# A gated mix of an S4 convolution and a dense layer, forward and backward, on one core: the order of the work around K's reload

## The chip, the cores and the metric

The kernel runs on one core of one Trainium2 chip. The metric is the time of one execution on the device, in microseconds (us). The engines are PE (matrix products; PEld is its weight load), DVE and ACT (elementwise work, and copies out of PSUM), POOL and SP (here almost only issuers of DMAs). Three queues issue DMAs: SP's, ACT's and POOL's. Each engine works through its own instructions in order.

## The reference

For a sequence `u` of 2048 rows of 448 channels the forward pass is a gate times a long convolution plus one minus the gate times a two-layer dense network, and the outputs are this result and the gradients of all inputs and weights:

```python
K = jnp.einsum("dn,dnl,dn->dl", Cc, P, dB).real      # P = exp(dt*A*l), 448 channels, 256 states, 2048 positions
Yf = rfft2(up) * rfft2(Kp)                           # zero-padded to 4096
y  = irfft2(Yf)[:L] + u * Dskip
h  = relu(x @ w1 + b1) ** 2
b  = h @ w2 + b2
out = g * y + (1 - g) * b                            # g = sigmoid(sum(u * gate_w))
_out, _vjp = jax.vjp(f, ...); grads = _vjp(grad_out)
```

## The kernel before

*FFT stage.* `u` and the gated gradient are transformed in two stages with matrix products: `fwd1` (line 222) writes its product to the DRAM buffer `gd`, `load_s1` reads it back transposed, `fwd2` (line 245) makes a spectrum, kept in DRAM as `sp_d`. `cmul` multiplies two spectra, `inv1` (line 272) is the first inverse stage and writes to `hd`; `load_hs` reads `hd` back, and `inv2` is the second inverse stage. `evac2` copies each product out of PSUM, half on ACT and half on DVE, or all on ACT while `act_only` is set. Between these, `powers` makes the tables from which K is built. A scheduler orders the instructions of this stage.

*Dense steps.* The dense layers are a generator (`dense`, line 896) of 196 steps: the first layer (`hidden`, `turn`, `mul_1`, 14 blocks of 128 features, four steps each), the second layer backward, the transposes of w1, and two projections (`project`, line 854: 16 rows of tiles, each in two half steps of 7 products, for each of two projections). `N_(n)` takes n steps; `D_(want)` takes steps until their summed costs reach `want`. The list `cost` gives each step a number.

*Chunks.* From line 957 on the order is the order of the code. K and its gradients are made in 14 chunks of 32 channels. A chunk is a list of tokens (`PERIOD`, line 1236): `YS`, `Y0` to `Y4` build a table Y on DVE, `KM` multiplies it on PE into 32 channels of K (`kgen`), `KO` copies them out and, after the last chunk, writes them to DRAM (`k_d`), `LY` transposes Y with four DMA transposes on SP, `X0` to `X2` build the other table, `Z0` to `Z3` are products on PE with the chunk before's transposed Y, each copied out by one ACT instruction, `P0` and `P1` products on DVE, `S` sums them on PE (`back_s`, 128 products into the PSUM tile psS) and writes them to `s_d` after every second chunk through a buffer `st`, `SA` and `WD` prepare weights. `D` stands for dense steps: the cost between the loop's start (`base`) and its end (`goal`) is spread evenly over all chunks, so that the last dense step runs just ahead of the last chunk's `KM`.

*Reload and tail.* After the last chunk `reload_k` loads K from `k_d` in rows by rounded position, 16 DMAs alternating between ACT's and POOL's queues. The small `fix` DMAs overwrite single rows of the `reload` ones and wait for them. `again` copies further rows on DVE. K then goes through `fwd1` (into `gd[2]`, with six stage buffers: four in the tile XB, two `st`), `load_s1`, `fwd2`; `product(w, q)` on DVE multiplies K's spectrum with that of the gradient (w = 0) or of `u` (w = 1), loaded from `sp_d` by `load_sx`, and `back1` is `inv1` of it, with four further stage buffers in the tile F. The products alternate between the tiles Pt and XB (`Pk`). A generator `param_grads` makes the parameter gradients in eight pieces for each of four channel blocks, taken by `Pg(n)`; its first block writes its results into XB. Two output loops end the kernel: out_0 (with `G`, the rows of grad_out, in the tile Y), and out_1.

Before the change the order at the end is: last `KM`, `KO`, `LY`, `P0`, `SA`, `reload_k`, `P1`, `S` of chunk 12, `WD`; loads of three spectra and of G's rows on SP; `Z0` to `Z3` of the last chunk (13); `again`; `P0`, `P1`; `fwd1` of K with the last chunk's sums between its parts; load of the constant `M2` into the tile M; `load_s1`.

## Time and profile before

| | |
|---|---|
| median of 3 runs | 879.25 us (879.04 to 881.17) |
| profiled execution | 882.18 us |
| its span, first to last instruction | 879.9 us |
| instructions | 20270 |
| busy share of the span: PE, PEld, DVE, ACT, POOL | 74%, 38%, 64%, 59%, 18% |
| mean granted clock of PE | 0.854 |
| moved by DMA | 181.58 MB, mean 206 GB/s |
| share of 16 DMA engines: SP's queue, POOL's, ACT's | 61.6%, 13.2%, 6.8% |

The profile is of one execution. Busy time is summed over instructions; PE's is partly modelled, since products are pipelined. In a row of the timeline come start and length in us, the engine (SPq and POOLq are the queues' own issuing work), the line, the operation, what it writes and reads, how many were merged (x), and in brackets how long the engine had stood before it and what ended that. The chain of waits gives start, length and what was waited for or done, followed back from the last instruction.

### The profile page before, as it was taken

What the parts mean: (1) busy time and instruction counts of PE and PEld (TensorE: products, weight loads), DVE (VectorE), ACT (ScalarE), POOL (GpSimd) and SP (SyncE); (2) the same over time, 40 slices, a digit from 0 to 9 for tenths busy, and PEclk for the clock granted to TensorE, in tenths of its full rate; (3) what the DMA queues carried; (4) which work ended last, traced back from release to release, by engine and by line L of the source; (5) the groups of instructions that cost most, each with busy time, mean ns of one, the idle gap of its engine ahead of it and who ended that gap; (6) DMA issues with size and microseconds to landing.
All of it is one profiled execution on the core that took longest, in us unless ns stands there. A gap on an engine that the chain in (4) does not pass through costs nothing.

```text
span 879.9 us, 20270 instructions
## 1 busy us (share of the span) xinstructions
PE 649.1 (74%) x8477; PEld 337.8 (38%) x8477; DVE 566.2 (64%) x932; ACT 515.5 (59%) x869; POOL 154.7 (18%) x260
## 2 busy tenths in 40 slices
PE   3578858777389987899999967988999151646382
PEld 1122323222244653556665643544656130323020
DVE  4595777975613573898889845475779151656574
ACT  1596787774166674587778737575454042656153
POOL 3122111105032011012111110100001132024142
PEclk9878976688699998999999986998999666879556
DMA  9957677587694889989998694985994997959892
GB/s 185 234 159 243 231 248 277 200 321 189 141 240 105 207 185 204 200 244 218 183 220 172 154 257 110 203 168 147 208 204 113 122 256 244 372 164 309 259 295 63
DMA packets 209545, 181.58 MB, mean 206 GB/s; under 512 B 132159, under 2 KB 185992, under 8 KB 209198
## 3 DMA queue, kind: packets, MB, share of 16 engines
q1 hardware_dynamic: 187822, 125.53, 61.6%
q0 software_dynamic: 13120, 34.18, 13.2%
q10 hardware_dynamic: 8512, 20.59, 6.8%
q8 instruction: 66, 1.08, 0.5%
q14 instruction: 25, 0.20, 0.1%
HBM read 85.19 MB, written 64.32 MB: 170 GB/s over the span
## 4 chain that ended last, share of the span: by engine, by line
PE 36%; DMA 19%; issue 15%; DVE 13%; ACT 12%; SPq 2%; POOL 2%; ACTq 0%; POOLq 0%; DVEq 0%
PE psN L876 8%; PE psN L683 5%; PE psN L647 5%; PE psS L1136 3%; PE psX L1064 3%; PE psF L1108 2%; DMA U<-rT_d 2%; DMA K<-dk_d 2%; DMA F<-rec_d 2%; PE psN L674 1%; DMA F<-k_d 1%; PE psN L650 1%; ACT U L675 1%; DMA K<-in_grad_out_dram 1%; DMA gd<-X 1%
## 5 line engine op out<-in xcount | busy, mean ns | idle before, releaser
L1110 ACT CAST P<-psF 128x1024 bf16<-128x1024 f32 x56 | 57.1, 1020 | 34.9 <-DMA F<-k_d 22.0
L1108 PE MATMUL psF<-S,R 41*128 41x32 bf16 x1792 | 32.0, 175 | 36.3 <-ACT P L1110 24.9
L683 PEld LDWEIGHTS <-U 128*128 128x128 bf16 x448 | 41.3, 101 | 39.5 <-issue 10.1
L647 PE MATMUL psN<-S 128*128 128x512 bf16 x168 | 48.2, 411 | 6.2 <-ACT st L1171 3.3
L683 PE MATMUL psN<-S,U 128*128 128x449 bf16 x224 | 51.3, 374 | 0.0
L1000 DVE TENSOR_TENSOR F<-Y,F 128x1024 bf16<-128x1024 bf16 (+3 forms) x70 | 47.2, 675 | 6.2 <-ACT F L1029 6.2
L999 DVE TENSOR_TENSOR Y<-Y,F 128x1024 bf16<-128x1024 bf16 (+3 forms) x70 | 48.0, 685 | 2.9
L1002 DVE TENSOR_TENSOR Y<-Y,F 128x1024 bf16<-128x1024 bf16 (+3 forms) x70 | 48.1, 687 | 2.4
L647 PEld LDWEIGHTS <-S 128*128 128x128 bf16 x336 | 30.1, 100 | 48.3 <-issue 22.2
L1108 PEld LDWEIGHTS <-R 41*128 41x128 bf16 x1792 | 27.4, 94 | 48.5 <-issue 39.8
L675 ACT ACTIVATE U<-psN 128x1024 bf16<-128x1024 bf16 x41 | 42.2, 1030 | 0.7 <-PE psN L674 0.7
L876 PE MATMUL psN<-D,U 128*128 128x448 bf16 x168 | 40.6, 395 | 2.6 <-ACT U L861 2.6
L876 PEld LDWEIGHTS <-U 128*128 128x128 bf16 x308 | 29.5, 103 | 33.2 <-issue 8.0
L662 ACT ACTIVATE U<-psN,b_f 128x512 bf16<-128x512 f32 x44 | 28.9, 685 | 19.3 <-PE psN L650 8.4
L989 DVE TENSOR_TENSOR R<-R,F 128x1024 bf16<-128x1024 bf16 (+1 forms) x14 | 13.4, 958 | 36.3 <-ACT R L1021 36.1
L1143 POOL DMA_DIRECT2D s_d<-st x28 | 14.5, 522 | 123.9 <-ACT st L1141 117.4
L253 PEld LDWEIGHTS <-M 128*64 128x64 bf16 x192 | 14.0, 127 | 55.2 <-issue 52.2
L647 PE MATMUL psN<-K,S 128*128 128x512 bf16 x126 | 33.3, 393 | 1.0 <-ACT R L768 0.7
L1119 DVE TENSOR_TENSOR M<-P,X 128x2048 bf16<-128x2048 bf16 x14 | 17.1, 1222 | 25.8 <-ACT P L1110 25.8
L1041 DVE COPY Y<-rec 128x256 bf16<-128x256 bf16 x14 | 10.2, 732 | 32.7 <-DMA K<-DBT_d 23.2
L1136 PE MATMUL psS<-ident,P 128*64 128x128 bf16 x896 | 28.3, 221 | 2.9 <-issue 2.9
L989 DVE TENSOR_TENSOR X<-X,F 128x1024 bf16<-128x1024 bf16 (+1 forms) x14 | 13.4, 959 | 23.4 <-ACT X L1021 21.1
(356 smaller groups left out, 1707.0 us busy)
## 6 DMA issues: line engine op xcount, KB each, us to landing
sp<-K ACTq DMA_DIRECT2D x8, 896.0 KB
R<-hd SPq DMA_DIRECT2D x14, 448.0 KB, 12.2
U<-rT_d SPq DMA_DIRECT2D x6, 896.0 KB, 5.9
hd<-F SPq DMA_DIRECT2D x11, 448.0 KB, 10.1
U<-rT_d SPq DMA_DIRECT2D x9, 512.0 KB, 6.4
X<-gd SPq DMA_DIRECT2D x5, 896.0 KB, 6.4
U<-dhT_d SPq DMA_DIRECT2D x5, 896.0 KB, 6.3
rT_d<-U POOLq DMA_DIRECT2D x8, 512.0 KB, 3.9
```

Source lines behind the costliest of these rows:

```text
L647: T_.matmul(pss[k][:], lhsT=w[:, dt], rhs=x(2 * half + k)[:, dt], start=(dt == 0), stop=False, skip_group_check=True)
L662: S.activation(r[:, 512 * lb:512 * lb + 512], pss[k][:], ACT.Relu, bias=b1_f[:, j:j + 1])
L675: S.activation(hn[j % 2][:, 8 * th:8 * th + 8, :], ps[:], f)
L683: T_.matmul(ps[:, 0:w], lhsT=hn[j % 2][:, t, :], rhs=rhs[:, t, :], start=(t == 0), stop=(t == LT - 1))
L876: T_.matmul(ps[:, 0:D], lhsT=src[:, j, P * x:P * x + P], rhs=ws[:, j, :], start=(w == 1 and j == 0), stop=(j == FT - 1))
L989: V.tensor_tensor(out=run(xb, 128 * n, [2048, 2], [W2, 2 * n], [1, W2]), in0=lo, in1=run(rx_[:, 0:1], 512 + W2 * k, [0, 2], [0, 2 * n], [1 ...
L999: V.tensor_tensor(out=run(yb, dst, [64, X2], [d0[1], n // d0[1]], [1, d0[1]]), in0=run(yb, 0, [64, X2], *src), in1=pr, op=ALU.mult)
L1000: V.tensor_tensor(out=run(vb, 0, [n, X2], [d0[1], n // d0[1]], [1, d0[1]]), in0=run(yb, 0, [64, X2], *src), in1=pi, op=ALU.mult)
L1002: return V.tensor_tensor(out=hi, in0=hi, in1=run(vb, n, [2 * n, W2], [-n, 2], [1, n]), op=ALU.add)
L1108: T_.matmul(psz[:, t, 32 * b:32 * b + 32], lhsT=yt[64 * t:64 * t + NY, b, :], rhs=DKc[64 * t:64 * t + NY, c % 2, 16 * (j % 2) + b].rearran ...
L1110: S.copy(run(zbs[c, h][:, 0:1], 16 * (j % 2), [1024, 2], [64, NA], [32, 2], [1, 16]), run(psz[:, 0, 0:1], 0, [512, 2], [1, NA], [NA, 2], [ ...
L1136: T_.matmul(sps[64 * h:64 * h + 64, cc, r, :], lhsT=Q[h][r][:, 1024 * t + 64 * a:1024 * t + 64 * a + 64], rhs=(nident if r == 0 and t == 1 ...
```

## The change

No instruction is added or removed, but the order and some buffers change.

- *Dense steps.* In the FFT stage the steps stand behind every second product of `fwd2` and behind each half of `inv1`, 36 of them and not 28. `TAILN` is 8: eight steps are kept for the time after the last chunk. The chunks get 16 fewer.
- *End of the loop.* All dense steps but eight are done ahead of the last `KM`; two spectra are loaded there on SP. Then `KM`, `KO`, the reload of K (on SP's and POOL's queues, not ACT's and POOL's), and behind it `LY`, `P0`, `SA`, `P1`, `S` of chunk 12, `WD`, and the eight dense steps.
- *K's first FFT stage* follows at once; `Z0` to `Z3`, `P0` and `P1` of the last chunk come behind it, and its sums in the first product loop. `M2` goes into the tile Y, ahead of the last two parts of this stage.
- *Tail.* G's rows are loaded in two halves, behind the third product of w = 0 and ahead of the products of w = 1. The first block's gradients go to the buffer `rec` and their pieces move from the products of w = 0 to those of w = 1. `Pk` changes its order, `load_hs` of w = 0 comes one step earlier for q = 0, parameters of block 1 are loaded behind the loops, u's rows behind all loads of `hd[2]`, and the product that needs them one turn later.

```diff
-    def fwd2(self, s1, q, out):
+    def fwd2(self, s1, q, out, between=None):
...
             self.evac2(out[:, ii], ps)
+            if between:
+                between(ii)
...
-    TAILN = 0
+    TAILN = 8
...
-            K.fwd2(s1, q, sp)
+            K.fwd2(s1, q, sp, lambda ii: N_(FW[ii]))
...
-            N_(NS1)
-    NS0, NS1, NS2 = 4, 2, 2
-    N_(NS0)
+    FW, IV = (0, 1, 0, 1), (2, 2)
+    N_(4)
...
-        K.inv1(Pc, q, hd[0])
-        N_(NS2)
+        K.inv1(Pc, q, hd[0], between=lambda q2: N_(IV[q2]))
...
-        (nc.scalar if xq % 2 else G_).dma_start(xs[p0:p0 + n, j:j + m]...
+        (nc.sync if xq % 2 else G_).dma_start(xs[p0:p0 + n, j:j + m]...
...
-    i = PERIOD.index("SA") + 1
+    i = PERIOD.index("KM")
     period(NCH - 1, PERIOD[:i])
+    D_(goal)
...
+    release()
+    assert done == total - TAILN
+    sx = {(0, 0): load_sx(0, 0, 5), (0, 1): load_sx(0, 1, 3)}
+    period(NCH - 1, ["KM", "KO"])
     reload_k()
-    period(NCH - 1, PERIOD[i:], PERIOD[:i].count("D"))
-    D_(goal)
-    assert done == total
+    period(NCH - 1, "LY P0 SA P1 S WD".split())
+    N_(TAILN)
     release()
...
-    for q, k in ((0, 4), (1, 5), (2, 3)):
-        sx[0, q] = load_sx(0, q, k)
-    load_rows16((nc.sync,), Gt, G2)
+    sx[0, 2] = load_sx(0, 2, 4)
...
-    for o in ("Z0", "Z1", "Z2", "Z3"):
-        period(NCH, [o])
...
-    period(NCH, ["P0", "P1"])
-    sums = back_s(NCH - 1, [Qs.pop((NCH - 1, h)) for h in range(2)])
...
+    M2v = Yf[:, 0:4096]
+    K.M2 = M2v
     def between(n):
-        if 0 < n < 6:
-            next(sums, None)
+        if n == 5:
+            nc.sync.dma_start(M2v, cdr["M2"].ap())
     K.fwd1(lambda j: xv[:, JO.index(j)], gd[2], stage=stg + [K.t("st", ...
-    M2v = P2[:, 0:4096]
-    nc.sync.dma_start(M2v, cdr["M2"].ap())
-    K.M2 = M2v
-    load_st(0, SB[:, 9856:11904], G_)
+    period(NCH, "Z0 Z1 Z2 P0 Z3 P1".split())
+    sums = back_s(NCH - 1, [Qs.pop((NCH - 1, h)) for h in range(2)])
...
-    for q in range(3):
-        sx[1, q] = load_sx(1, q, q)
+    for w, q, k in ((0, 3, 0), (1, 0, 1), (1, 1, 2)):
+        sx[w, q] = load_sx(w, q, k)
-    obs[0] = XB[:, 0:1536]
+    obs[0] = rc[:, 0:1536]
-    Pg(1)
...
-    Pk = [... for b in (Pt, XB)]
+    Pk = [... for b in (XB, Pt)]
...
             K.fwd2(s1k[q + 1], q + 1, spk(q + 1))
+        if q < 2:
+            sx[1, 2 + q] = load_sx(1, 2 + q, (5, 3)[q])
+        for _ in range(6):
+            next(sums, None)
         back1(0, q)
-        if q > 0:
-            Pg((0, 2, 2, 3)[q])
-        if q < 2:
-            sx[(0, 3) if q == 0 else (1, 3)] = load_sx(q, 3, 4 + q)
-    load_raw(1, SB[:, 3584:5120], G_)
-    load_st(1, SB[:, 9856:11904], G_)
+        if q == 2:
+            load_st(0, SB[:, 9856:11904], G_)
+            Pg(1)
+            load_rows16((nc.sync,), Gt, G2, (0,))
+    hs1.append(load_hs(1, 0, 6))
+    load_rows16((nc.sync,), Gt, G2, (1,))
     for q in range(4):
         product(1, q)
-        hs1.append(load_hs(1, q, (3, 6, 4, 0)[q]))
+        Pg((2, 2, 2, 1)[q])
         back1(1, q)
+        if q < 3:
+            hs1.append(load_hs(1, q + 1, (4, 0, 1)[q]))
...
+    load_raw(1, SB[:, 3584:5120], G_)
+    load_st(1, SB[:, 9856:11904], G_)
...
-        hs2.append(load_hs(2, q, (1, 2, 5, 3)[q]))
-        if q == 1:
+        hs2.append(load_hs(2, q, (2, 5, 3, 6)[q]))
+        if q == 3:
             load_rows16((nc.sync,), Uv, u2)
...
-        if q == 1:
+        if q == 2:
             psr = K.ps("X", [P, 512])
```

More of the change, by code (lines that the diff above doesn't have):

```diff
@@ L291, in inv1 @@
             self.q3.dma_start(dst, st[:])
+            if between:
+                between(q2)
     def load_hs(self, hd, q, hs):
@@ L339, with load_rows16 @@
     K = Ker(tc, pool, psum)
-    def load_rows16(queues, dst, ap2d):
+    def load_rows16(queues, dst, ap2d, halves=(0, 1)):
         for g in range(NG):
-            for h in range(2):
+            for h in halves:
                 src = bass.AP(tensor=ap2d.tensor, offset=ap2d.offset + (16 * g + 8 * h) * D, ap=[[64 * D, 32], [1, 8 * D]])
@@ L1313, in fix @@
         xq += 1
-        (nc.scalar if xq % 2 else G_).dma_start(xs[p0:p0 + step * (n - 1) + 1:step, j], bass.AP(tensor=k_d, offset=row * D, ap=[[st_ * D, n], [1, D]]))
+        (nc.sync if xq % 2 else G_).dma_start(xs[p0:p0 + step * (n - 1) + 1:step, j], bass.AP(tensor=k_d, offset=row * D, ap=[[st_ * D, n], [1, D]]))
     def reload_k():
@@ L1473 @@
     K.st_more = oq
-    Pk = [b[:, 0:7168].rearrange("p (k a r d) -> p k a r d", k=2, a=4, r=2) for b in (Pt, XB)]
+    Pk = [b[:, 0:7168].rearrange("p (k a r d) -> p k a r d", k=2, a=4, r=2) for b in (XB, Pt)]
     def product(w, q):
```

21 lines of the change are left out of this document (10 added, 11 removed).

## The prediction

> **What bounds the kernel now.** I read the table of stages first (busy time of each engine between two moments), because the page's averages (PE 74%, DVE 64%, ACT 59%) hide stages with different limits.
>
> ```profile
> 60.00:205.00 145.00, 109.16 (x543) 40.35 (x543) 106.30 (x219) 106.13 (x188) 24.82 (x40) 0.78 0.71 246
> ...
> 271.00:681.90 410.90, 368.47 (x6426) 222.01 (x6427) 291.87 (x399) 268.82 (x423) 40.93 (x71) 0.95 0.85 184
> 681.90:713.00 31.10, 6.15 (x256) 5.58 (x254) 8.72 (x16) 5.50 (x6) 5.15 (x9) 0.64 1.07 159
> 713.00:746.30 33.30, 14.44 (x160) 7.37 (x160) 9.87 (x14) 9.90 (x17) 11.57 (x20) 0.71 0.87 248
> 746.30:782.00 35.70, 20.64 (x160) 9.97 (x161) 17.74 (x16) 23.59 (x47) 2.19 (x4) 0.83 0.90 327
> 782.00:821.10 39.10, 20.12 (x175) 9.98 (x175) 23.73 (x21) 17.68 (x33) 12.73 (x23) 0.81 0.80 253
> ```
>
> The columns are start and end, length, busy time (and instructions) of PE, PEld, DVE, ACT and POOL, the granted clock, the DMA share and GB/s. From 60 to 205 us (FFT stage) PE, DVE and ACT are each busy about 75% (109, 106, 106 of 145): no engine is the bound, they hand work to each other, at clock 0.78. From 271 to 681.9 (the 14 chunks with the dense steps) PE is busy 368.5 of 410.9, 90%, at clock 0.95: PE is the bound. From 681.9 on it is not: 6.15 of 31.1 us while K is reloaded, 14.4 of 33.3 in K's first FFT stage. There the DMA share is 0.8 to 1.07.
>
> Four chunks, each from the end of one kgen to the end of the next, show how even the loop is:
>
> ```profile
> 321.60:363.10 41.50, 30.11 (x509) 17.39 (x510) 23.52 (x35) 22.87 (x37) 4.72 (x9) 0.92 1.05 199
> 392.20:422.10 29.90, 29.12 (x527) 18.09 (x528) 25.18 (x36) 23.70 (x42) 5.00 (x9) 1.00 0.93 189
> 507.10:557.10 50.00, 35.85 (x519) 20.61 (x523) 26.41 (x36) 29.87 (x39) 3.31 (x6) 0.80 0.84 185
> 655.00:681.90 26.90, 26.90 (x488) 16.57 (x488) 21.33 (x28) 13.39 (x21) 2.97 (x5) 1.00 0.60 124
> ```
>
> A usual chunk has PE full (29.1 of 29.9; 26.9 of 26.9) with DVE behind (25.2, 21.3). Two are long: 41.5 us with 11.4 idle, and 50.0 with 14.2 idle. The first hole is this:
>
> ```profile
> 321.43 24.05 SPq L1083 DMA_TRANSPOSE R<-Y  x4
> ...
> 345.65 0.97 SPq L756 DMA_DIRECT2D U<-rT_d  x2
> ```
>
> Four transposes of Y hold SP for 24 us, and the load of rT that PE's next layer needs is behind them on the same queue.
>
> Next the end, in the timeline, for who waits:
>
> ```profile
> 648.93 10.74 SPq L1083 DMA_TRANSPOSE R<-Y  x4
> ...
> 681.95 0.53 ACT L1071 CAST X<-psX 128x328 bf16<-128x328 f32 x1 [1.50 <-PE psX L1064]
> ...
> 683.96 18.40 SPq L1083 DMA_TRANSPOSE R<-Y  x4
> 685.13 0.70 POOL L1075 DMA_DIRECT2D k_d<-X  x1 [1.66 <-issue]
> ...
> 690.56 1.33 POOL L1308 DMA_DIRECT2D F<-k_d  x2 [4.72 <-DMA k_d<-X]
> ...
> 702.81 0.53 POOL L1314 DMA_DIRECT2D F<-k_d  x1 [10.92 <-DMA F<-k_d]
> ...
> 703.34 1.97 POOL L1308 DMA_DIRECT2D F<-k_d  x4
> ...
> 713.08 0.53 PE L232 MATMUL psN<-F,cb_F1BD 128*128 128x448 bf16 x1 [2.46 <-DMA F<-k_d]
> ...
> 714.72 0.49 POOL L1314 DMA_DIRECT2D F<-k_d  x1 [9.41 <-PE psN L232]
> ...
> 720.63 4.18 SPq L237 DMA_DIRECT2D gd<-X  x4
> ...
> 722.69 0.36 PE L232 MATMUL psN<-F,cb_F1BD 128*128 128x448 bf16 x1 [1.78 <-DMA F<-k_d]
> ...
> 734.49 0.53 ACT L206 CAST st<-psN 128x448 bf16<-128x448 f32 x1 [7.92 <-DMA s_d<-st]
> ...
> 746.34 0.83 SPq L243 DMA_DIRECT2D K<-gd  x2
> ...
> 782.26 2.03 DVE L1479 TENSOR_TENSOR X<-U,S 128x3584 bf16<-128x3584 bf16 x1 [8.46 <-DMA out_dram<-X]
> ...
> 821.14 0.68 DVE L1532 SCALAR_TENSOR_TENSOR F<-psN,g,K 128x448 bf16<-128x448 f32 x1 [11.42 <-issue]
> ```
>
> and in the chain of waits, for the landings:
>
> ```profile
> 685.13 4.66 DMA k_d<-X
> ...
> 691.27 11.26 DMA F<-k_d
> ```
>
> K's last chunk goes to DRAM (landed 689.8), is reloaded in three links, each waiting for the one before: 690.6 to 702.5; 703.3 to about 713; and one row alone, 714.7 to 722.7. The first link takes 11.26 us where the write before it took 4.66, and it lands as SP's four transposes end (683.96 + 18.40 = 702.4). PE starts K's first FFT stage (line 232) at 713.1, 31.2 us after kgen's end. That stage then loses 7.9 us at 734.5, because its buffer `st` is being written to s_d by the last chunk's sums, and its product is first read back at 746.3. Further on DVE stands 8.5 us at 782.3 (a product into XB waits for parameter gradients leaving XB) and 11.4 us at 821.1, for which the profile names no releaser; by the code its output goes into the buffers from which hd's last writes leave.
>
> **The change, part by part.** No instruction is added or removed; every step moves. So I price what each move takes from one stage and gives to another.
>
> *Dense steps: eight into the FFT stage.* They are steps of the first layer, two of every four being rows like these of the chain:
>
> ```profile
> 278.17 0.55 PE psN L674 x8
> 278.73 1.51 PE psN L683 x8
> 280.24 1.29 PE psN L647 x6
> 281.53 0.32 PE psN L650 x2
> ```
>
> Turn 0.55, product 1.51, hidden layer 1.29 + 0.32: 3.67 us for two steps, 14.7 for eight at full clock. In the changed program's order three such pairs (11.0 us) come to stand ahead of the last inverse of this stage; the other two steps fall behind it, where PE waits for DMAs anyway. At clock 0.78 the 11.0 are 14.1. Cover is PE's idle quarter; if that were gone, all 14.1 would be paid. ACT gets six bias-relu and three squares:
>
> ```profile
> L662 ACT ACTIVATE U<-psN,b_f 128x512 bf16<-128x512 f32 x22 | 14.9, 681 | 9.8 <-DVE st L531 6.2 <-DVE st L218 2.3 <-PE psN L650 1.1
> ...
> L675 ACT ACTIVATE U<-psS 128x1024 bf16<-128x1024 bf16 x9 | 9.1, 1012 | 0.0
> ```
>
> 6 x 0.681 + 3 x 1.012 = 7.1 us, into 39 us of idle ACT. Lower bound 0 (36 us of PE are idle here), upper 14.1. An instruction put at random into an engine that is 75% busy delays it for three quarters of its length, and these are laid between the waits of two other engines, so my estimate takes the row's 0.75: **+11**.
>
> *The loop loses sixteen steps.* Eight of the first layer, 14.7, and eight of the last projection, each half of 14 products:
>
> ```profile
> 677.12 2.75 PE psN L876 x14
> ```
>
> 4 x 2.75 = 11.0. Together 25.7 us of PE, spread by cost over 13 chunks: 2.0 a chunk. After it PE has 27.1 in a usual chunk against DVE's 25.2, so PE stays the bound, narrowly. Bounds: -25.7 if every PE microsecond counts, -10 if the two holes and the DVE-tight chunks eat over half. PE's share is 0.90, and I take off a little more for DVE, 0.8: **-20**.
>
> *The reload.* The other eight steps now run behind kgen and the sums of chunk 12, which follow kgen as before; a chunk's sums are this row:
>
> ```profile
> 659.10 3.69 PE psS L1136 x128
> ```
>
> 11.0 + 3.7 us of PE, ending about 16 us after kgen with the waits between them. They are free as long as the reload takes longer. It does. Counting from kgen's end: copy 0.5, POOL's second write of K issued at 3.2, landed at 7.9 with the old 4.66 (two loads of u's spectra are ahead of it now, in place of the transposes). First link: issue 0.8, landing bounded by 4.66 (the write of the same K) and 11.26 (the same load among transposes); no transposes are in flight, so 4.66, done at 13.4. SP's part then waits for it, so the transposes behind it start at about 16. Second link: 1.97 us of issue and 4.66, at 20: the FFT stage starts there and not at 31.2. Third link: 8 us as now, ending 8 us after the start, as now (9.6).
>
> What is queued behind these waits on SP: four transposes, one load, then every second write of the FFT stage. The transposes take 10.74 (row of 648.93) to 18.40, so SP is free at 27 to 34; I take 31, 11 us after the FFT stage began; before, its first write from SP went out 7.5 us after the start (720.63). That costs 3.4. The old stage lasted 33.3 us to the read-back; without the 7.9 of `st` (the sums now come later) 25.4; 20 + 25.4 + 3.4 = 49 against 64.4: **-15**. Bounds: -21 (transposes 10.74, write of M2 unseen) and -4 (second link 11.26, transposes 18.40). Z0 to Z3, P0 and P1 of the last chunk now stand behind this stage:
>
> ```profile
> L1110 ACT CAST P<-psF 128x1024 bf16<-128x1024 f32 x56 | 57.1, 1020 | 34.9 <-DMA F<-k_d 22.0
> ...
> L1119 DVE TENSOR_TENSOR M<-P,X 128x2048 bf16<-128x2048 bf16 x14 | 17.1, 1222 | 25.8 <-ACT P L1110 25.8
> ```
>
> Four evictions of 1.0 us and four products of 1.2 us, 9 us with PE's part, lie between the stage's last eviction (about 42) and the first spectrum read back (issue at 49 and some 5 us of landing). If the read-back came at once, they would cost up to 9.
>
> *XB no longer shared.* The gradients go to `rec`, and their steps move into the second product loop: the 8.46 us at 782.3 go, **-8.5**. The sums enter the first loop (3.7 us of PE, where PE has 15 of 35.7 us idle): nothing. Without that cover 3.7.
>
> *G's rows move* from the reload, where DMA had room behind the transposes, into the product loops, 8 x 224 KB = 1.8 MB, 5.5 us at the 327 GB/s of 746 to 782, where the share is 0.90. The raw parameters and sums of block 1 (0.9 MB) leave them. Net 2.8 us, **+3**; 0 if the 20% idle share of 782 to 821 holds it. The 11.4 us at 821.1 stay: the same six stage buffers, the same writes behind loads on SP. The output loops stay as they are; u's rows go behind all loads of hd, and their user goes one turn later.
>
> Sum: 11 - 20 - 15 - 8.5 + 3 = -29.5. The profiled execution lasted 882.2 us, 2.3 more than its span; 852.7. It stands 2.9 above the median of the runs, 879.25, so **850**.
>
> **Rivals.**
>
> B, *the transposes keep their price*. The second link and the FFT writes still meet four transposes, now 5 us later than the link's issue. The link takes 11.26 (+6.6), SP is free at 34 or later (+4): 850 + 10.6 = 861. For it: POOL's part and the last row are not ahead of the transposes on their queue. Against: the second link has 5 us of head start, what the write needed. A rule of the Trainium skill speaks for B ("DMA: Bandwidth & Descriptors", section "Queues, rings and completion order"): a DMA engine takes turns between the queues that have work, packet by packet. By it the old reload, on ACT's and POOL's queues, was not shut out by SP's transposes, getting ahead of them gains little, and the sum is B's 861; the landing at 702.5, just as they ended, does not look like turns.
>
> C, *the FFT stage takes its eight steps for nothing and the loop gives all sixteen back*: +0 and -25.7, 850 - 11 - 5.7 = 833. For it: 36 us of idle PE against 14, and an order laid out finer (a step behind every second product). Against: no engine there is slack by itself. The Trainium skill ("TensorE: Matmul & The Clock Gate", Part 1) says the array is throttled by default and some 3.4 us of sustained work release it: a fuller PE would then run its 109 us faster than at 0.78, which is C or better. The trace agrees in direction, 0.78 at 75% busy and 0.95 at 90%.
>
> D, *slower: a load behind four transposes*. All dense steps shift against the chunks, so loads on SP meet the transposes in other places. Price: the chunk of 321.6 lasted 41.5 against 29.9, 11.6 us each. From the third new one (34.8 against 29.5) the change loses: three give 885. For it: in the changed order one load of the projection's rows stands behind the transposes where it stood ahead. Against: the two loads of the hole at 345.65 now stand ahead of them, so one is won.
>
> **Chances and range.** My forecast 0.52, B 0.20, C 0.16, D 0.10 and, between D and none, 0.02 for no change. The forecast's own spread is 838 to 861. All bounds at their best give 0 - 25.7 - 21 - 8.5 = -55, 824; at their worst 14 - 10 - 4 - 8.5 + 3 = -5.5, 874. I cut both ends a little: 828 to 872 leaves out D and the far tail of C, some 0.15. Within 0.3% (2.6 us) a measurement of this kernel cannot tell a change. Faster 0.88, same 0.02, slower 0.10.
>
> **What would show it.** FFT stage: the last write of hd (line 291's) issued 11 us later than now. Loop: kgen's last end at 681.9 + 11 - 20, some 673, PE still at 90% or more. Reload: K's first FFT matmul 20 us behind kgen's end; 31 means that the transposes still hold it. Read-back of gd 49 us behind kgen; no wait on s_d, none on XB. The second step of the first output loop 119 us behind kgen (139.2 now). I am wrong if the loop shows new holes with SP's transposes ahead of a load, if the FFT stage grows by over 14 us, or if SP, held by the reload's waits, is the last to end in front of the read-back.

## The result, and the profile after

The changed kernel takes 858.8 us (median of 4 runs, 854.1 to 868.9) against 879.1 of the kernel before in the same job: 20.3 us less; the ratio is 0.975 (95% interval 0.970 to 0.979). Ratios here leave out the few slow executions, over 1.5% above the fastest of the same kernel (the 868.9 is one). The forecast was 850.0, range 828 to 872. The profiled execution took 860.13 us, its span is 858.4 (before: 882.18 and 879.9). The total lies inside the range; its distribution over the stages does not follow the forecast. Stages are read from the one profiled execution of each kernel. "Behind kgen" is measured from the end of the last kgen, which falls at 681.8 before and 664.3 after; "the tail" is what follows it. (The loop's row counts to the last product as its tile lists it, 0.2 us earlier.) "The second step" of the first output loop is its first write of an output, the row at L1539 below. The last column has the other executions of which the program is the same up to that moment.

| us | before | forecast | after | same order, other runs |
|---|---|---|---|---|
| first kgen starts (price of the FFT stage's steps) | 258.0 | 269 | 266.3 | 265.4 to 272.7 |
| loop, first kgen to last | 423.6 | 403.6 | 397.8 | 398 to 408 |
| K's first FFT matmul, behind kgen | 31.3 | 20 | 21.2 | 20.8 to 21.5 |
| first read-back of gd, behind kgen | 64.5 | 49 | 57.8 | 55.4 to 56.7 |
| second step of the first output loop, behind kgen | 139.3 | 119 | 134.9 | 133.5 |
| end, behind kgen (the tail) | 198.1 | 177.6 | 194.1 | 192.6 |

So the loop gave 25.8 us where 20 were forecast, the FFT stage cost 8.3 and not 11, and the tail gave 4.0 us of the 20.5 that were counted on. Together -21.5, the difference of the spans.

The table of stages of the changed kernel (start and end, length, busy time of PE, PEld, DVE, ACT and POOL, granted clock, DMA share, GB/s):

```profile
60.00:205.00 145.00, 111.61 (x557) 42.10 (x563) 103.04 (x216) 108.66 (x193) 24.96 (x42) 0.79 0.69 242
266.30:664.30 398.00, 347.46 (x6431) 216.14 (x6463) 297.10 (x408) 262.88 (x413) 42.28 (x74) 0.94 0.90 193
664.30:685.50 21.20, 14.81 (x186) 9.04 (x184) 6.43 (x15) 3.64 (x6) 5.38 (x9) 0.94 0.57 135
685.50:722.10 36.60, 12.00 (x160) 5.84 (x161) 13.53 (x17) 11.85 (x18) 8.73 (x15) 0.59 0.97 216
722.10:754.00 31.90, 24.70 (x292) 13.96 (x292) 17.96 (x12) 22.82 (x45) 2.80 (x5) 0.86 0.91 350
754.00:776.00 22.00, 14.37 (x132) 7.08 (x133) 21.79 (x20) 16.63 (x33) 6.42 (x12) 0.98 0.89 230
776.00:799.20 23.20, 5.67 (x43) 2.42 (x40) 1.81 (x7) 3.71 (x7) 8.45 (x15) 0.65 1.06 308
799.20:822.30 23.10, 14.43 (x72) 3.03 (x72) 19.45 (x57) 3.83 (x12) 6.44 (x12) 0.50 0.90 255
822.30:858.40 36.10, 22.82 (x108) 5.07 (x106) 20.77 (x44) 17.80 (x39) 13.38 (x25) 0.59 0.53 156
```

and of the kernel before, the loop and the last two stretches, which the prediction did not show:

```profile
258.00:681.80 423.80, 380.06 (x6616) 228.65 (x6616) 298.70 (x409) 275.04 (x431) 45.02 (x78) 0.95 0.85 185
821.10:843.90 22.80, 14.10 (x71) 2.90 (x70) 19.16 (x56) 3.83 (x12) 6.44 (x12) 0.50 0.86 236
843.90:879.90 36.00, 19.82 (x112) 4.83 (x108) 21.07 (x47) 17.69 (x39) 13.39 (x25) 0.64 0.54 157
```

Read the next to last column. From 685.5 to 822.3 the DMA share is 0.89 to 1.06 in every stretch, while from 776 to 799 PE works 5.7, DVE 1.8 and ACT 3.7 of 23.2 us. Share times length, summed over the tail, measures the work of the DMA engines (the share is counted from the times of packets and can pass 1): 12.1 + 35.5 + 29.0 + 19.6 + 24.6 + 20.8 + 19.1 = 160.7 us after, and 164.7 before (33.3 + 29.0 + 32.1 + 31.3 from the prediction's four rows, 19.6 + 19.4 from these). What is left of the tail, 33.4 and 33.3 us, is the same. So are the bytes: GB/s times length gives 45.7 MB after and 45.8 before.

The timeline of the changed kernel shows what became late in place of what was removed:

```profile
673.02 1.34 POOL L1310 DMA_DIRECT2D F<-k_d  x2 [4.55 <-DMA k_d<-X]
679.41 0.53 POOL L1316 DMA_DIRECT2D F<-k_d  x1 [5.04 <-DMA F<-k_d]
681.85 17.07 SPq L1085 DMA_TRANSPOSE R<-Y  x4
685.54 1.65 PE L232 MATMUL psN<-F,cb_F1BD 128*128 128x448 bf16 x4 [6.05 <-DMA F<-k_d]
...
699.02 2.46 SPq L1340 DMA_DIRECT2D U<-sp  x1
701.59 2.81 SPq L237 DMA_DIRECT2D gd<-X  x4
...
709.28 0.97 ACT L206 CAST X<-psN 128x448 bf16<-128x448 f32 x2 [15.67 <-DMA gd<-X]
709.30 1.16 DVE L207 CAST X<-psN 128x448 bf16<-128x448 f32 x2 [14.85 <-DMA gd<-X]
...
722.09 0.80 SPq L243 DMA_DIRECT2D K<-gd  x2
...
799.21 0.68 DVE L1539 SCALAR_TENSOR_TENSOR F<-psN,g,K 128x448 bf16<-128x448 f32 x1 [18.04 <-DMA hd<-F]
```

and its chain of waits has the landings:

```profile
703.83 7.29 DMA gd<-X
...
712.30 9.52 DMA gd<-X
...
768.74 10.96 DMA hd<-F
...
782.18 16.93 DMA hd<-F
```

K's write and its links wait 4.55 and 5.04 us, and K's first FFT matmul runs at 685.5. Then DVE and ACT stand 15 us for stage buffers: the writes of gd from SP are behind four transposes and one load, the first goes out at 701.6, and the landings take 7.3 and 9.5 us. At the end of the tail DVE's wait for `hd<-F`, 11.4 us before, is 18.0.

### The profile page after: what moved, and what is told of

Its sections match the earlier page's. It is cut to its first block, busy times and chain, and to the rows that moved or that the text cites. A ratio compares the mean times of both kernels' runs of the same rounds, so it can differ in the third digit from the quotient of the medians.

```text
span 858.4 us, 20221 instructions
## 1 busy us (share of the span) xinstructions
PE 642.5 (75%) x8433; PEld 337.7 (39%) x8477; DVE 565.5 (66%) x932; ACT 514.1 (60%) x869; POOL 155.8 (18%) x262
## 4 chain that ended last, share of the span: by engine, by line
PE 35%; DMA 22%; DVE 14%; ACT 14%; issue 9%; SPq 3%; POOL 1%; ACTq 0%; POOLq 0%; DVEq 0%
PE psN L880 7%; PE psN L651 5%; PE psS L1138 4%; DMA R<-Y 3%; DMA hd<-F 3%; PE psX L1066 3%; PE psN L687 2%; DMA U<-rT_d 2%; SPq L1085 2%; DMA gd<-X 2%; DVE Y L1001 2%; PE psF L1110 1%; PE psX L687 1%; DVE F L1002 1%; DMA F<-rec_d 1%
## 5 line engine op out<-in xcount | busy, mean ns | idle before, releaser
L687 PE MATMUL psN<-S,U 128*128 128x449 bf16 x224 | 47.9, 355 | 0.0
L880 PEld LDWEIGHTS <-U 128*128 128x128 bf16 x308 | 29.1, 102 | 32.1 <-issue 8.0
L679 ACT ACTIVATE U<-psN 128x1024 bf16<-128x1024 bf16 x37 | 38.1, 1031 | 1.3 <-PE psN L678 1.3
L666 ACT ACTIVATE U<-psN,b_f 128x512 bf16<-128x512 f32 x44 | 28.6, 685 | 14.7 <-DVE st L535 7.5
L687 PE MATMUL psX<-D,U 128*128 128x448 bf16 x144 | 36.0, 391 | 0.7 <-ACT D L693 0.7
L232 PEld LDWEIGHTS <-cb_F1BD 128*128 128x128 bf16 x96 | 10.3, 117 | 55.2 <-issue 45.4
L651 PE MATMUL psN<-K,S 128*128 128x512 bf16 x99 | 27.9, 394 | 4.8 <-issue 3.5
L865 ACT ACTIVATE U<-U 128x1792 bf16<-128x1792 bf16 x12 | 20.1, 1694 | 15.7 <-DMA U<-rT_d 15.7
L880 PE MATMUL psN<-S,U 128*128 128x448 bf16 x140 | 28.4, 353 | 0.0
```

Source lines behind the costliest of these rows:

```text
L651: T_.matmul(pss[k][:], lhsT=w[:, dt], rhs=x(2 * half + k)[:, dt], start=(dt == 0), stop=False, skip_group_check=True)
L666: S.activation(r[:, 512 * lb:512 * lb + 512], pss[k][:], ACT.Relu, bias=b1_f[:, j:j + 1])
L679: S.activation(hn[j % 2][:, 8 * th:8 * th + 8, :], ps[:], f)
L687: T_.matmul(ps[:, 0:w], lhsT=hn[j % 2][:, t, :], rhs=rhs[:, t, :], start=(t == 0), stop=(t == LT - 1))
L880: T_.matmul(ps[:, 0:D], lhsT=src[:, j, P * x:P * x + P], rhs=ws[:, j, :], start=(w == 1 and j == 0), stop=(j == FT - 1))
```

## The experiments

Each diff is against the changed kernel. Ratios are to the kernel before, in the same job.

*The mark.* The changed kernel once more.

> The changed kernel again, as the mark for the others of this group. Theory and rivals alike: 0.97 to 0.98 of the kernel before; the last kgen ends near 664, K's first FFT matmul is 21 us behind it, the first read-back of gd 58, the second step of the first output loop 135, the end 194. A mark that moves by more than 3 us here can't carry a verdict in the other runs.

862.9 us, 0.980 (0.974 to 0.986); loop 401.5, tail 192.6. The median moved by 4.1 us, more than the limit named, and the span of the profiled execution by 2.9, with 3.7 more in the loop. So edits in the tail are judged from kgen's end on, where the mark moved by 1.5; a difference of 2 us there says little.

*Other queue for gd's writes.*

```
-   (self.q2 if g2 == 0 else nc.sync).dma_start(dst, st[...])      # fwd1
+   (self.q2 if g2 == 0 else self.q4).dma_start(dst, st[...])      # q4 = nc.scalar for K's fwd1
```

> In K's first FFT stage the half of gd's writes that SP issued is issued by ACT; everything else as changed. Theory (the queue): the 15.67 us wait of ACT and 14.85 of DVE in this stage is only the writes standing behind four transposes on SP. Then this wait is under 4 us, the eight writes are out before the transposes end, and the first read-back of gd, which is still behind the load of M2 on SP, comes 43 to 47 us behind kgen's end, not 58. If the rest of the tail follows, the end comes 11 to 14 us earlier (845 to 847). Rival 1 (shared engines): transposes hold any write, whatever its queue: the wait stays above 10 us and the end within 3 us of the mark. Rival 2 (the tail is set later, by hd's last writes): the read-back comes at 43 to 47, but the wait on hd at the first output loop grows by as much, and the end gains under 5 us.

860.9 us, 0.976 (0.972 to 0.980). SP and ACT in the timeline:

```profile
687.02 23.09 SPq L1086 DMA_TRANSPOSE R<-Y  x4
...
718.58 0.58 ACTq L237 DMA_DIRECT2D gd<-X  x1
719.20 1.01 ACT L1113 CAST P<-psF 128x1024 bf16<-128x1024 f32 x1 [10.29 <-DMA R<-Y]
```

The long wait on gd is gone as the theory had it, but the four transposes, next to the writes now, hold SP for 23.09 us and not 17. The read-back (at 724.0) is 54.7 behind kgen, 2 us before the mark's 56.7; the tail is 190.4, 2.2 less. Rival 1 was wrong about the wait and right about the end.

One write still waits for the transposes. The last of ACT's eight goes out at 718.58, though the last copy into its buffer ended at 708.9. In the trace it uses the same completion counter (semaphore 113) as the fourth transpose, so ACT stands until that transpose has landed: this is the wait of 10.29 us in the row of 719.20. SP's wait ahead of the read-back lasts from 719.2 to 723.8 for this write alone. These 4.6 us belong to the counters that the program shares out, not to the DMA engines, so the run leaves open what a queue free of them would gain.

The Trainium skill ("DMA: Bandwidth & Descriptors", section "Issuing engines are not separate DMA queues") says that, whichever engine starts a DMA, it runs on the same 16 DMA engines among the others, and a second issuing engine saves only the time of issuing. The trace agrees in direction, 23.09 us of transposes against 17.07.

*Parameters later.* Blocks 1 to 3 are loaded in the first output loop.

```
-        if q == 2:
-            load_raw(2, SB[:, 6272:7808], G_)
-            load_st(2, SB[:, 7808:9856], G_)
-    load_raw(1, SB[:, 3584:5120], G_)
-    load_st(1, SB[:, 9856:11904], G_)
-    load_raw(3, SB[:, 0:1536], G_)
-    load_st(3, SB[:, 1536:3584], G_)
...
         hs2.append(load_hs(2, q, (2, 5, 3, 6)[q]))
+        if q < 3:
+            load_raw(q + 1, SB[:, (3584, 6272, 0)[q]:][:, 0:1536], G_)
+            load_st(q + 1, SB[:, (9856, 7808, 1536)[q]:][:, 0:2048], G_)
```

> The parameters and sums of blocks 1 to 3 (0.9 MB each, on POOL's queue) are loaded one block per step of the first output loop, not while the last writes of hd are under way. Theory (contention): these loads stretch the last writes of hd to 10.96 and 16.93 us in the chain of waits. Without them the second one takes 6 to 9 us, DVE's wait of 18.04 us at the start of the first output loop is 8 to 11 us, and its second step stands 125 to 128 us behind kgen (135 as changed); the loop grows by up to 2 us with the loads in it; the end comes 6 to 9 us earlier. Rival (bytes): the stretch has no idle DMA time and SP's own loads of hd and writes fill it: the wait stays above 15 us or the output loops give the gain back, and the end is within 3 us of the mark.

864.0 us, 0.980 (0.973 to 0.987). DVE, then ACT in the timeline:

```profile
800.49 0.68 DVE L1532 SCALAR_TENSOR_TENSOR F<-psN,g,K 128x448 bf16<-128x448 f32 x1 [13.81 <-DMA hd<-F]
...
834.99 0.91 ACT L216 CAST F<-psF 128x896 bf16<-128x896 f32 x1 [5.55 <-DMA out_dram<-F]
...
844.01 0.53 ACT L206 CAST F<-psN 128x448 bf16<-128x448 f32 x1 [4.62 <-DMA out_dram<-F]
```

DVE's wait shrinks from 17.6 (mark) to 13.81, and the loop's second step comes 4 us earlier (129.3 behind kgen). The second output loop then waits 5.55 and 4.62 us for outputs to leave its buffers, and the tail is 193.8: all given back, as the rival said. The theory's 8 to 11 us of wait and 6 to 9 us of gain did not come.

*Other output buffers*, twice: the second time the last loop takes its buffers one later.

```
-   ao = oq[q]
+   ao = aq[q]      # aq: XB[:, 2048:3840], XB[:, 3840:5632], Pt[:, 4608:6400], oq[0]
...
-   xo = oq[q]
+   xo = oq[(q + 1) % 4]      # in the second run only
```

> The first three steps of the first output loop write into other buffers (parts of XB and Pt that are free by then), the fourth into the first stage buffer; nothing else moves. Theory (a buffer, not data): DVE's 18.04 us wait is for stage buffers whose writes to hd have not landed, and nothing in the loop needs those rows of hd. Then the wait goes and the loop's second step stands about 118 us behind kgen. The second output loop reads the last rows of hd[2], whose writes land at about 799 and whose loads need some 6 us more, so the end gains less than the 17 us: the second loop can start at about 806 at the earliest where it started at 822, and the end comes 8 to 14 us earlier. Rival (data): the loop's later steps or its first loads of hd wait for the same DMA time: another wait of 10 us or more stands in the first loop, and the end is within 3 us of the mark.

> As the run with other output buffers in the first output loop, but the second loop takes the stage buffers in an order that starts one later, so that its first step does not wait for the last write of the first loop (11.67 us of ACT there). Theory (buffers): the second loop starts once the last rows of hd[2] are loaded, 148 to 151 us behind kgen instead of 156, and the end comes 5 to 8 earlier than in that run: tail 182 to 186. Rival (DMA work): the rows of hd, u's rows and the outputs still have to pass; the second loop's first step comes no earlier than 154 behind kgen, or later steps wait instead, and the tail stays at 189 or more.

858.3 us, 0.974 (0.969 to 0.980), and 863.9, 0.980 (0.973 to 0.986). ACT and DVE of the first:

```profile
782.66 0.68 DVE L1540 SCALAR_TENSOR_TENSOR X<-psN,g,K 128x448 bf16<-128x448 f32 x1
...
822.64 0.53 ACT L206 CAST F<-psN 128x448 bf16<-128x448 f32 x1 [11.67 <-DMA out_dram<-F]
```

and ACT of the second:

```profile
812.32 0.53 ACT L206 CAST F<-psN 128x448 bf16<-128x448 f32 x1 [3.24 <-issue]
...
840.72 0.52 ACT L1570 CAST rec<-psX 1x448 bf16<-1x448 f32 x1 [9.93 <-PE psX L1569]
```

The 18 us wait is gone (second step at 115.7 and 115.6 behind kgen), so it was for buffers and not for data. In the first run the time comes back at 822.6, by my choice of the fourth buffer; in the second the last loop starts at 147.5 behind kgen, about as expected, and then stands at 840.7 for a product of u's rows, whose loads are behind those of hd. Tails 190.4 and 191.2: 17 us off one wait, some 2 off the end. The gain of 8 to 14 us and the tail of 182 to 186 that were expected did not come; the ends are those of the rivals.

*Bytes left out.* G's rows (1.8 MB) and the parameters and sums of blocks 1 to 3 (2.3 MB) are not loaded; what uses them reads stale values.

```
-            load_rows16((nc.sync,), Gt, G2, (0,))
...
-    load_rows16((nc.sync,), Gt, G2, (1,))
...
-        for i, a in enumerate((A_A_re, ..., A_C_im)):
+        for i, a in enumerate((A_A_re, ..., A_C_im) if dt == 0 else ()):
...
-        q_.dma_start(b[:z, 0:2048].bitcast(fp32)...
+        if dt == 0: q_.dma_start(b[:z, 0:2048].bitcast(fp32)...
```

> The changed kernel without the loads of G's rows (1.8 MB, both halves) and of the parameters and sums of blocks 1 to 3 (2.3 MB): stale values are read in their place, everything else is issued as before. Theory (the tail is set by the work of the DMA engines: from K's first FFT stage to the second output loop their share is 0.89 to 1.06 in every stretch, and share times length over the whole tail is 165 us before the change and 161 after): 4.1 MB at the 308 to 327 GB/s of these stretches are 13 us; DVE's 18 us wait at the start of the first output loop falls under 6, and kgen's end to the end of the kernel takes 178 to 183 instead of 193. Rival (order: the hd writes are late because of what is ahead of them on SP's queue and of the buffers they leave, not because of bytes): the wait stays above 12 and the tail above 188.

848.4 us, 0.962 (0.956 to 0.967). The tail's stages:

```profile
674.30:695.60 21.30, 14.82 (x186) 9.05 (x184) 6.39 (x15) 3.64 (x6) 5.46 (x9) 0.94 0.57 135
695.60:729.70 34.10, 11.95 (x160) 5.83 (x161) 13.49 (x17) 11.85 (x18) 8.72 (x15) 0.60 0.96 232
729.70:765.00 35.30, 27.15 (x324) 15.47 (x324) 21.64 (x14) 26.34 (x51) 2.79 (x5) 0.89 0.89 336
765.00:792.60 27.60, 15.66 (x143) 7.27 (x139) 19.93 (x24) 16.55 (x33) 3.23 (x6) 0.99 0.97 274
792.60:817.00 24.40, 15.71 (x78) 3.27 (x78) 19.62 (x58) 4.88 (x16) 7.71 (x15) 0.50 0.88 245
817.00:849.70 32.70, 21.31 (x102) 4.78 (x100) 20.61 (x43) 16.86 (x36) 12.02 (x23) 0.60 0.56 163
```

and DVE at the start of the first output loop:

```profile
792.63 0.68 DVE L1537 SCALAR_TENSOR_TENSOR F<-psN,g,K 128x448 bf16<-128x448 f32 x1 [5.57 <-issue]
```

The wait is 5.57 us and the tail 175.4, 17 to 19 us shorter, with the order of all else as it was (178 to 183 were expected). The DMA engines' work, summed as above, is 142.8 us: 17.9 less than the 160.7, and the rest is 32.6. So the DMA work sets the tail: here it is that work plus some 33 us in which the engines are idle, 9 of them in the 21 us behind kgen and 17 in the last 36. Two limits of this reading: the loads that are left out also leave their places in SP's and POOL's queues, and the run does not part the two; and the rest is no constant, it is 29 us with the parameters later and 27 in the control below.

*Transposes into the idle time*, and a control with SP's half of the reload on ACT, so that the transposes start at kgen's end.

```
-   period(NCH - 1, PERIOD[:i])                                  # ends "Y4 D"
+   period(NCH - 1, PERIOD[:i - 1] + ["LY", "D"])                # first kernel
...
-   sx = {(0, 0): load_sx(0, 0, 5), (0, 1): load_sx(0, 1, 3)}
    period(NCH - 1, ["KM", "KO"])
    reload_k()
-   period(NCH - 1, "LY P0 SA P1 S WD".split())
+   sx = {(0, 0): load_sx(0, 0, 5), (0, 1): load_sx(0, 1, 3)}
+   period(NCH - 1, "P0 SA P1 S WD".split())
...
-   (G_ if c == 9 or g % 2 == 0 else nc.sync).dma_start(k_d...)
+   (G_ if c == 9 or g % 2 == 0 else nc.scalar).dma_start(k_d...)
...
-   (nc.sync if xq % 2 else G_).dma_start(xs...k_d)              # second kernel
+   (nc.scalar if xq % 2 else G_).dma_start(xs...k_d)
```

> The last chunk's four transposes are issued ahead of the last dense steps and of kgen (their table is ready some 1.5 us before), SP's half of the write of K goes to ACT, and the two early loads of spectra go behind the reload. In the 21 us after kgen the DMA share was 0.55 to 0.57, the 9 us that are idle there are the only ones ahead of the output loops. Theory (DMA work): the transposes use them, SP is free for gd's writes, the waits of 14 to 16 us in K's first FFT stage fall under 5, the read-back of gd stands 46 to 50 us behind kgen (57 in the runs so far) and the end comes 6 to 9 earlier (tail 184 to 187, not 193). Rival 1 (the chain of K): its write and first link run among the transposes again, as before the change; the write and the links take up to 6.6 us more each, K's first FFT matmul stands 26 to 31 behind kgen and the end gains under 3. Rival 2 (the later stretch is full anyway): the read-back is at 46 to 50 but the wait at the first output loop grows from 18 to 24 or more, and the end gains under 3.

> The half of K's reload that SP issued is issued by ACT, as before the change; the order is the changed one. So SP starts the transposes at once, while K is written and reloaded. Theory (DMA work, as the run with early transposes showed: they fill idle DMA time, K's chain is stretched by a few us, and the tail shrinks): K's first FFT matmul 24 to 28 behind kgen, no wait over 5 us on gd, read-back at 48 to 52, tail 184 to 188. Rival (the transposes shut the reload out, as they seemed to before the change): first link 11 us or more, matmul at 30 to 33, read-back at 54 or later, tail 190 or more.

858.5 us, 0.973 (0.967 to 0.979), with the transposes early; 856.5, 0.973 (0.967 to 0.979), in the control. Stages of the first, and its transposes:

```profile
675.30:699.20 23.90, 14.67 (x188) 9.07 (x184) 6.42 (x15) 3.75 (x6) 5.42 (x9) 0.87 0.84 133
699.20:723.20 24.00, 11.83 (x160) 5.75 (x161) 13.53 (x17) 11.94 (x18) 8.69 (x15) 0.64 0.89 314
723.20:760.00 36.80, 27.91 (x330) 15.79 (x331) 23.08 (x15) 27.78 (x54) 2.79 (x5) 0.90 0.92 339
760.00:799.60 39.60, 15.44 (x137) 6.96 (x132) 18.49 (x24) 15.20 (x31) 14.81 (x27) 0.82 0.97 273
799.60:858.70 59.10, 37.05 (x179) 8.05 (x178) 40.23 (x101) 21.63 (x51) 19.73 (x37) 0.56 0.70 196
```

```profile
671.90 13.44 SPq L1085 DMA_TRANSPOSE R<-Y  x4
```

and K's chain in the control, on POOL:

```profile
677.46 1.34 POOL L1310 DMA_DIRECT2D F<-k_d  x2 [6.98 <-DMA k_d<-X]
686.21 0.53 POOL L1316 DMA_DIRECT2D F<-k_d  x1 [7.41 <-DMA F<-k_d]
...
695.09 0.49 POOL L1316 DMA_DIRECT2D F<-k_d  x1 [6.37 <-DMA F<-k_d]
```

With the transposes early the 21 us behind kgen become 23.9 at a share of 0.84 and not 0.57; the waits for gd's buffers in K's first FFT stage are under 3 us, the read-back is at 47.9 and the tail 183.4: DMA work 155.1 and 28.3 idle. The theory holds; the tail is even shorter than the 184 to 187 expected, and the wait at the first output loop (17.75 us) did not grow as rival 2 had it. The profiled kgen ended at 675.3, since the FFT stage was the slowest of all (first kgen at 272.7), and the whole time shows less of the gain. The order of instructions up to there is the same; yet the other kernel with early transposes (*Together*) has 271.7 and the other nine with 36 steps 265.4 to 269.0. Whether this is chance is open. In the control K's write and links wait 6.98, 7.41 and 6.37 us among the transposes, not 11; K's first matmul comes 7.4 us later than with the change (28.6 behind kgen) and the read-back 3.5 earlier (53.2), the tail is 190.3. Theory and rival both miss: the tail is the rival's (190 or more), the matmul and the read-back lie between the two. Neither side shut the other out, and K's chain, 7 us later, cost nothing that shows at the end.

*The dense steps put back*: the eight of the tail, the eight of the FFT stage, both.

```
-   TAILN = 8
+   TAILN = 0
...
-   FW, IV = (0, 1, 0, 1), (2, 2)
+   FW, IV = (0, 1, 0, 1), (0, 2)
```

> The eight last dense half steps go back into the loop, none stands behind the last kgen. Theory (in the loop every microsecond of PE counts; under the reload they are free): 4 x 2.75 = 11.0 us. First kgen to last kgen took 397.7 to 404.9 in the five executions of the changed order (423.6 before the change); here 408 to 416, the tail stays at 191 to 194, the end 9 to 12 later. Rival 1 (the loop has room, its gain came from another alignment of loads and transposes): the loop stays under 404 and the end within 3. Rival 2 (the dense steps in the tail cost something, PE or ACT are late for K): the tail shrinks by 4 or more and the end is only 4 to 7 later.

> The eight steps added to the FFT stage go back into the loop (28 there as before the change); the eight behind the last kgen stay. The loop's chunks showed that the one of 41.5 us before the change is 29 to 31 after it, which is half of the loop's gain of 19 to 26, and that eight last steps put back cost the loop nothing. Theory A (PE time): first kgen at 256 to 260 (266 to 273 with the change), the loop takes 14.7 more, 411 to 418, the end is 3 to 8 later than the mark. Theory B (place of the loads): what the loop gained is the hole where the second layer's first rows stood behind four transposes; with the old pace of the first layer it comes back: one of the first four chunks takes 40 or more and the loop 415 to 424. Theory C (room): the loop stays under 408 and the end comes 5 to 9 earlier, the FFT stage having taken the steps at 9 us for nothing.

> The dense steps as before the change (28 in the FFT stage, none behind the last kgen), with all the rest of the change. With only eight of the sixteen put back, either way, the loop took 402.0 and 403.2 us, against a mean of 400.6 with the change, where eight steps are 11 to 14.7 us of PE. Theory (two limits: with all sixteen in it PE's work is the bound and the load behind the transposes opens its hole; with any eight out another limit, near 400 us, takes over): the loop takes 417 to 425 with one of its first four chunks at 40 or more, the first kgen is at 258 to 263, the tail 190 to 194, and the end is 872 to 878, 0.985 to 1.0 of the kernel before. Rival (the loop's gain is from something else in the change, such as the order of its last loads, and not from the steps): loop 400 to 408, end 855 to 862.

The eight of the tail back: 865.5 us, 0.982 (0.975 to 0.988). The eight of the FFT stage back: 857.4, 0.973 (0.968 to 0.979). Both: 876.2, 0.990 (0.983 to 0.997). The loop in each, in this order, from the tables of stages:

```profile
267.80:670.00 402.20, 365.81 (x6522) 222.05 (x6524) 298.20 (x409) 264.94 (x417) 42.73 (x74) 0.94 0.90 195
```

```profile
262.40:665.80 403.40, 363.52 (x6560) 221.64 (x6562) 298.51 (x409) 272.59 (x427) 44.22 (x77) 0.96 0.90 196
```

```profile
261.10:685.40 424.30, 378.12 (x6584) 230.52 (x6618) 298.53 (x409) 274.95 (x431) 45.37 (x78) 0.94 0.86 189
```

Lengths of the 13 chunks, from one copy of K out of PSUM to the next:

```
before          29.8 31.8 41.5 29.1 29.9 30.6 27.8 31.3 45.7 36.0 34.7 26.8 26.9   421.8
after           30.2 33.6 29.0 33.1 27.1 27.8 26.3 26.8 42.2 31.4 36.1 26.8 25.5   395.9
tail's back     26.3 35.5 30.1 32.3 29.3 28.1 27.5 37.3 37.0 35.1 26.9 25.5 29.1   400.1
FFT stage's     29.1 28.6 40.4 30.1 29.8 29.2 28.7 28.1 40.3 33.9 29.0 25.9 28.2   401.4
both back       30.9 31.7 41.8 27.5 29.8 30.6 27.8 30.9 47.7 39.2 30.5 26.8 26.8   422.2
```

The hole in the third chunk of "both", and the same place with the change, on SP's queue:

```profile
325.18 24.88 SPq L1085 DMA_TRANSPOSE R<-Y  x4
350.23 0.98 SPq L760 DMA_DIRECT2D U<-rT_d  x2
```

```profile
317.51 2.24 SPq L760 DMA_DIRECT2D U<-rT_d  x2
325.81 16.73 SPq L1085 DMA_TRANSPOSE R<-Y  x4
```

With all sixteen back the loop is the old one, 424.1, with the old hole, and the end (0.990) is where the theory had it; the tail is 190.9. Eight out, whichever, gives 402 or 403; the second eight, 11 or 14.7 us of PE, give 1 to 2 more (401.1 in the mean of the ten executions with the change, which spread from 397.7 to 408.0: the 1 to 2 can't be told from nothing). So the first run went as its rival 1 (room in the loop); the second has theory B's hole and theory C's length. PE's busy time falls from 365.8 and 363.5 to 347.5, and its idle time rises from 36.4 and 39.9 to 50.5: they became idle time. The hole is a matter of place: with the change the loads of rT go out at 317.5, ahead of the transposes, and in "both" at 350.2, behind 24.9 us of them. Yet the run with the FFT stage's steps back has that hole (40.4) and the short loop, so the hole is not the whole. DMA share times length is 358 to 365 us in all five loops, and the share 0.90 in the three short ones; that the DMA engines are the limit near 400 fits this, but no run took bytes out of the loop, so it stays open.

For the kernel's time this says where most of the gain comes from: with the sixteen steps back in their old places the kernel takes 0.990 of the time before, and with the whole change 0.975 or 0.980.

The FFT stage's price: with 28 steps the first kgen is at 262.4 and 261.1, with 36 at 267.8 in the mean of eleven executions (265.4 to 272.7): some 6 us for eight steps.

*Together.* Early transposes and the other output buffers, as in their diffs above; and the product of u's rows behind the last step, with half of out_1's writes on ACT's queue:

```
-   if q == 2:  psr = ...                                         # product of u's rows
+   if q == 3:  psr = ...
-   nc.sync.dma_start(dst, xo...)
+   (nc.scalar if q < 2 else nc.sync).dma_start(dst, xo...)
```

> Three edits at once: the last chunk's transposes ahead of the last dense steps; the first output loop's other buffers with the second loop's order one later; and the product that needs u's rows behind the last step of the second loop, with half of the writes of out_1 on ACT's queue (in the run with other buffers PE stood 9.8 us there, waiting for u's rows, with the rest of the loop behind it). Theory: tail 183.4 in the run with early transposes, less 6 to 10 for the second loop that starts 10 us earlier and no longer stands: 173 to 178, 0.955 to 0.965 of the kernel before. Rival (DMA work again: u's rows land as late, and the writes of out_1 behind them): the tail is 181 or more.

855.2 us, 0.968 (0.962 to 0.973); tail 181.6, DMA work 154.8 and 26.8 idle: 1.8 us better than the early transposes alone, and not the 6 to 10 of the theory; it is the rival's tail (181 or more). PE, in the timeline, still stands for u's rows:

```profile
834.69 5.14 PE L1569 MATMUL psX<-K,ds_b 128*1 128x448 bf16 x16 [4.87 <-DMA K<-in_A_u_dram]
```

It is the best ratio of the kernels that compute everything; its interval overlaps that of the changed kernel's first measurement (0.970 to 0.979) by 0.003 and lies below the mark's.

## Why the prediction was right, and where not

The sign was right. That the total lies in the range is in part luck: a tail that fell short by 16.5 us was half made good by a loop and an FFT stage that came out better than forecast. By the prediction's own steps:

- *Dense steps into the FFT stage, +11*: right in kind. The first kgen came 8.3 us later (8.3 for the last write of hd too, where 11 were named), some 6 us of it by the runs with the steps put back. The forecast was three quarters of 14.1 us; by those runs the price is nearer half.
- *The loop, -20*: right in size, wrong in reason. The step that failed is "I take off a little more for DVE, 0.8": the price is not a share of PE's time, and PE did not stay the bound (its share fell from 0.90 to 0.87). Of two times eight steps the first eight taken out give 21 to 22 us, more than their 11 or 14.7 of PE, and the second no more than the spread of the executions. What the limit near 400 us is stays open. The hole that closed was named in rival D ("one is won") but priced in no term.
- *The reload, -15*: measured -6.7 (57.8 against 64.5). K's chain went as forecast, 7.9, 13.4, 16 and 20 us behind kgen against 8.1, 14.7, 17.6 and 21.2. The step that failed is "That costs 3.4", for SP behind the transposes. I put a delay of SP's first write, 3.5 us, in place of a wait for all of them. The first write went out 16.1 us after the stage's start, where 11 were taken: the transposes held SP for 17.07 us, near the upper bound, and the load behind them, which the sum left out, for 2.5. The landings took 7.3 and 9.5 us, and two engines stood 15. By the prediction's own sign of being wrong, SP was the last to end in front of the read-back: its write of 712.30 landed at 721.8. The run on ACT's queue shows that the queue is not all of it: without that wait the read-back gains 2 us, and at most some 5 more if the shared counter is taken off. The sum counted engine waits in a stretch whose DMA share is 0.97.
- *XB, -8.5, and G's rows, +3*: read-back to the second step of the first output loop took 74.8 before and 77.1 after, +2.3 and not -5.5. No wait on XB is left, as forecast. The work moved: DVE is busy 21.8 of 22 us from 754 to 776, with the gradients' pieces, and the stretch behind it waits for DMA. "The 11.4 us at 821.1 stay" was wrong: they became 18.0.
- *Output loops, 0*: 59.2 us from the second step on, against 58.8. Right.

In the prediction the DMA shares of 0.8 to 1.07 in the tail stood in the first table, and the text used them for where PE is not the bound. Priced by DMA work, of which the change removes none (the bytes are the same), the tail's forecast would have been near 0; 4.0 us were measured. The errors were +16.5 in the tail, -5.8 in the loop and -2.7 in the FFT stage: 8.0 us in the end. The 0.3% below which a change could not be told was too narrow: executions of the changed kernel lie between 854 and 869 us.

Rival B, that the transposes keep their price, gave 861, closest of all, by another way than what happened: the second link did not meet them (K's matmul at 21.2), the FFT stage's writes did. Its rule, that the engines take turns between queues (the Trainium skill, "DMA: Bandwidth & Descriptors", section "Queues, rings and completion order"), agrees with the control, where link and transposes share at 7.41 us, between the 5.04 without transposes and the 10.92 of before. Rival C's half on the loop came true (-25.8), its half on the FFT stage did not; the clock there was 0.79 against 0.78 with PE busy 111.6 and 109.2 of 145. A fuller PE that is clocked higher, as C took it from "TensorE: Matmul & The Clock Gate" in the Trainium skill, Part 1, is not seen in this stage; PE is hardly fuller, so this is no test of it. Rival D fell: the kernel did not get slower, and the one change of place that showed was a gain.

## What to carry to other kernels

Multiply DMA share by length over each stretch before and after a move: here, where the sum stayed and the share was near 0.9, engine waits that were removed came back as other waits, and what shortened the tail was fewer bytes, or bytes moved into a stretch with idle DMA time. The sum is no count of bytes: a share of 0.97 went with 216 GB/s in K's first FFT stage and one of 0.91 with 350 GB/s behind it. When a write goes out late, look also at what its completion counter was used for last. Ask of each stretch which of its shares is at its limit, and price a move there by that resource alone. Work taken from a stage at its limit need not pay in proportion: take its parts out singly to see where it stops paying.

## What the runs showed of the hardware

- Four DMA transposes of Y (2.1 MB) held SP for 13.4 us when issued early (671.90 above), 15.0 to 17.6 in K's stage, 23.1 there beside the writes of gd, and 24.9 in one chunk of the loop (325.18). They land later than SP's row ends: beside the writes of gd SP was free at 710.1 and the fourth landed at 718.5.
- An execution's loop, with the same program up to that point, varied from 397.7 to 408.0 us, and the FFT stage's end by 7 us; medians of one kernel in two jobs differed by 0.005 in ratio (0.975 and 0.980).
- PE's granted clock was 0.50 in the first output loop (14.4 us busy of 23.1, after 20.6 us without a product) and 0.98 from 754 to 776 (14.4 of 22.0): the busy share is nearly the same, 0.62 and 0.65, and the clock is not.
